# A new written order for five engines: first loads, transpose banks and the low parts of w_down in a two-layer transformer kernel

## The chip, the core and the metric

The kernel runs on one core of one Trainium2 chip. The metric is the device time of one execution in microseconds (us). The engines are TensorE (PE, with its weight loads as PEld), VectorE (DVE), ScalarE (ACT), GpSimd (POOL) and SyncE (SP), which issues the DMA transfers. Each engine works through its own list of instructions in order; semaphores make an instruction wait for data of another engine.

## The reference

Two layers, run twice with the same weights, on 2048 positions of 512 numbers, all fp32:

```python
def _A_ref(x, wqkv, wo):                    # H = 32 heads of Dh = 16
    q, k, v = split(x @ wqkv)               # wqkv: 512 x 1536
    idx = pos[:, None] - arange(8)[None] * 2 # 8 earlier positions, every second one
    logits = einsum("bhsd,bhswd->bhsw", q, k[idx]) * Dh ** -0.5   # masked where idx < 0
    o = einsum("bhsw,bhswd->bhsd", softmax(logits), v[idx])
    return o @ wo                           # wo: 512 x 512

def _B_ref(x, w_gate, w_up, w_down):        # 512 x 1792, 512 x 1792, 1792 x 512
    return (gelu(x @ w_gate) * (x @ w_up)) @ w_down

for _ in range(2):
    x = x + _A_ref(layernorm(x), wqkv, wo)
    x = x + _B_ref(layernorm(x), w_gate, w_up, w_down)
```

(The loop and the names of the split are shortened here.)

## The kernel before

**Arithmetic.** A product of fp32 matrices is made from f16 matmuls: each operand is split into a high part (the number rounded to f16) and a low part (what the rounding left), and three products high x high, high x low and low x high are added in PSUM. Weights are scaled first by a power of two, for which the largest magnitude of the weight is needed: `absmax` on DVE (L719) or `abssum` on ACT (L731) over each tile as it is loaded, then `exponents` (L615 on), which takes a turn over PE (a transpose, L628) and a few tiny DVE operations (L621, L638 to L643), then `power` (L659, L662). After that `split` makes the high part on ACT (L675) and the low part on DVE (L680). w_q has eight tiles, four for each half h of the heads; w_g and w_u have eight tiles each. The tensor names in the profile stay with a buffer, so weights that are staged elsewhere appear as w_d, bx or sc.

**w_down.** The product with w_down is done in seven block products in place of eight (a scheme of Strassen's kind). For that, `prep_d` makes seven blocks of the weight for each of seven groups u: sums on DVE (L861 to L864), a cast to f16 on ACT (L883) and the low parts on DVE (L886). For u = 0 to 4 a low part is one subtraction of 1792 elements per partition, for u = 5 and 6 two of 896.

**Stages.** The 2048 positions are eight chunks of two tiles (128 positions each), per layer. For a chunk: x tiles are loaded (L989 for the first chunk's two tiles, L971 for others), their statistics are taken on DVE (`norm`, L1035 and L1039) and finished on POOL (L1090 to L1107), ACT writes the normed tile (L1155), ACT casts the high part (L1117) and POOL subtracts the low part (L1121), and both are transposed, on PE for the first tiles (L1136, copied out of PSUM by ACT at L1143), else by a DMA of SP's (L1126). PE multiplies the transposed tile ax with w_q (L1205; for each tile and half twelve matmuls of 512 columns and twelve of 256), ACT evicts (L1231) and SP stores to a scratch in HBM (L1240), from which it fetches q and the shifted k and v (L1270). Attention is on DVE: q times k (L1293), its sum (L1302), softmax, weights times v (L1360), its sum o (L1372). o is split, transposed, multiplied with wo (L1166) and added to x (L1409). Then the feed-forward layer: norm, split, transpose (bx and hl in the profile), two matmuls (L1166), gelu on ACT (L1460), the product on DVE (L1467), block sums on POOL (L1480, L1482), cast on ACT (L1506), low part on POOL (L1511), the down product on PE (L1520), and the sums to the output on DVE (L1551). Projections of later chunks are put in front of the first feed-forward block and, later, between the blocks.

**PSUM.** During the start the pool `P_pg` for projections has six banks and the pool `P_pt` for transposes one. Some of these banks are later handed over to the accumulation of the down product; `retire` keeps them from being taken anew:

```python
P_pg = Pool(
    "pg", [ps.tile([P, 512], F32, name=f"pg{i}") for i in range(3)] + banks(pds[0], pds[1], pds[3]),
    fifo=False,
)
P_pt = Pool("pt", banks(pds[2]), fifo=False)
```

**What sets the order.** Each operation is a node of a graph (`Graph.add`), with the engine it runs on, what it reads and writes and the buffers that it takes. Nodes are numbered as they are added. `SEQ` holds a list of these numbers for each of the five engines: this list, and nothing else, is the order in which the engine issues. `Graph.plan` walks through the lists with a model of the engines' costs, to settle which buffer of a pool a node gets; it cannot change the order. Priorities and earliest times (`prio=`, `after=`) are left over from an earlier search and do not order anything here. Between the start's real work PE has a few matmuls that nobody reads (`unread`, L1594).

At the start SP's list loads four w_q tiles of half 0 first; the two x tiles of chunk 0 are its 8th and 11th transfer.

Of the kernel before, what the change touches and what calls it, by code (L numbers as in the profile page):

```python
# [39 lines left out]
    for tiles in TILES  # L40
# [15 lines left out]
    xl=-1044.97, gu=12.98, early=1, xin=554.42, wait=0.01, zero=-1577.82, dl=0, ds=0, pds=1216.47, late_end=90.68,  # L56
# [11 lines left out]

G_AT = {3: 0, 6: 1, 7: 2, 4: 3, 1: 4, 2: 5, 5: 6}
# [6 lines left out]
        17 227 228 225 226 38 96 263 271 231 298 232 230 270 229 272 274 273 275 277 276 278 279 281 280 268 282-287  # L76
        289 288 291 293 290 292 324 67 297 299 300 302 304 301 303 325 306 308 504 305 307 511 509 512 309-313 315
# [12 lines left out]
        1592 1593 1603 1604 1612 1611 1762 1620 1764 1619 1629 1599-1602 1610 1637 1630 1638 1618 1646 1645 1628  # L90
# [14 lines left out]
    """,  # L105
    "DVE": """
        13 9 16 30 18-20 240 28 34 26 250 22 24 251 241 489 491 37 492 490 58 95 39 60 59 97 40 41 63 98 64 65 45 61
        62 119 122 43 66 120 124 68 123 125 69 121 126 72 74 47 76 78 49 80 82 127 84 688 86 689-691 885 70 886 129
        340 130 131 341 135 133 342 137 887 139 888 343 141 344 143 145 345 1080 369 147 370 1081 346 176 371 1082
        178 1083 179 372 1275 182 373 348 1276 349 374 375 184 350 1277 187 1278 351 1470 352 1471 189 353 357 192  # L110
        1472 207 1473 358 1665 359 194 377 197 378 210 379 380 199 220 1667 1666 1668 381 202 382 204 386-388 213
        214 217 537 538 394 223 396 224 539-543 566 545 567 546-550 568-570 421 571 554 555 572 556 574-577 432 578
        440 579 583 584 448 450 585 736 458 737 738 591 739 593 740 764 741 765 466 474 743-748 766 482 767 483 618
        484 752 768 485 769 486 753 629 754 487 931 771 637 932 647 645 772 1860 773 1862 1863 1861 774-776 655
        780-782 933 663 934-936 959 671 960 788 790 938 961 939 940 962 963 941 942 964 943 679 680 947 681 948 682
        949 683 966 684 1126 815 1127 2057 967 2059 2058 968 826 2060 969-971 834 975-977 842 844 1128 852 1129 983
        1130 985 1154 1131 1155 1133-1137 860 1138 868 1142-1144 876-878 1156 1010 1157 879 880 1158 881 1159 1021
        1161-1164 1029 2254 2256 2255 1165 2257 1166 1039 1037 1170-1172 1321 1047 1322 1323 1055 1324 1178 1325
        1349 1326 1180 1350 1351 1063 1352 1328 1329 1353 1330-1332 1354 1333 1071 1337 1072 1338 1073 1339 1074
        1075 1356 1076 1357-1361 1365-1367 1516 1205 2449 2451 2450 2452 1517 1216 1518 1224 1519 1373 1544 1520  # L120
        1375 1545 1521 1234 1232 1523-1528 1546 1242 1547 1532 1250 1533 1548 1534 1258 1549 1711 1712 1551-1554
        1400 1411 1266 1555 1267 1268 1419 1269 1427 1429 1270 1271 1437 1445 1453 2644-2647 1461-1466 1556 2839
        1560 2840 1561 1562 1713-1715 2841 1716 2842 1739 1718 1740 1568 1719-1722 1570 1723 1741-1743 1727 1744
        1728 1729 1746-1751 1755-1757 1595 1906 1606 1907 1908 1614 1909 1763 1910 1935 1765 1936 1622 1937 1624
        1938 1939 1911 1632 1912 1940 1941 1640 1914-1917 1648 1918 1919 1923-1925 1656 1657 1943 1944 1658 1945
        1790 1659 1660 1946 1661 1801 1947 1948 1952 1953 1809 3034 3036 3035 3037 1954 1819 1817 2103-2105 1827
        1960 1962 2106 2132 1835 2133 2107 2134 2108 1843 2135 2109 2136 2137 2111 2138 2112-2116 2120 1851 1852
        2121 1853 1854 2140 1855 1856 2141 2142 2122 2143 3229 2144 3230 1987 2145 3231 2149 3232 1998 2150 2151
        2006 2300 2014 2016 2301 2302 2024 2303 2157 2328 2159 2329 2032 2304 2330-2332 2305 2040 2333 2307-2312
        2316-2318 2048 2335 2049 2336 2050 2337 2051 2338 2184 2052 2053 2339 2340 2195 2344-2346 2203 2495 2496  # L130
        2211 2213 2497 2498 2354 2499 2500 2523 2221 2524 2502 2503 2525 2526 2352 2504 2505 2229 2506 2507 2527
        2511 2512 2237 2528 2513 2530-2535 2245 2539 2246 2540 2247 2541 2248 2690 2249 2691 2250 2692 2693 2379
        2694 2718 2547 2390 2719 2695 2720 2398 2721-2723 2549 2697 2698 2406 2699 2700 2408 2701 2702 2706 2707
        2416 2708 2885 2725 2886 2726 2727 2424 2432 2728-2730 2734-2736 2887 2440 2574 2888 2441 2442 2889 2443
        2585 2913 2914 2444 2445 2593 2915 2916 2742 2744 2917 2890 2918 2601 2603 2892-2897 2901 2902 2611 2619
        2920-2922 2903 2627 2923-2925 2929 2930 2635 2931 2636 2637 2769 2638-2640 3080 2780 3081 3082 2788 3083
        2937 2939 3108 3084 3109 3085 2796 2798 3110 3087 3088 3111 3089 3112 3090 3113 2806 3091 3092 3096 2814
# [1524 lines left out]
```

## Time and profile before

| | |
|---|---|
| time, median of 3 | 1239.27 us (1238.78 to 1241.88) |
| the profiled execution | 1239.04 us |
| its span, first to last instruction | 1237.3 us |
| PE busy | 1198.5 us (97%) |
| DVE, POOL, ACT busy | 941.3 (76%), 666.8 (54%), 539.1 us (44%) |
| granted clock, mean | 0.991 |
| HBM | 115.87 MB read, 33.73 MB written |

The profile gives for each engine its busy time, for each group of instructions (line, engine, operation, tiles) the busy time, the mean of one, and the idle time in front of them with the engine whose signal ended it. A timeline row reads: start, duration, engine, line, operation, out<-in with partitions x elements, and in brackets the idle time before it. Times within the span count from its first instruction.

### The profile page before, as it was taken

The page shows a single profiled execution, that of the slowest core. Times are in us where ns is not written, and L with a number is a line of the kernel's source. Part 1 is how long each engine was busy: PE and PEld are TensorE (multiplying, and loading weights), DVE is VectorE, ACT ScalarE, POOL GpSimd, SP SyncE. Part 2 cuts the span into 40 slices and gives each one's busy share as a digit, 9 for nine tenths or more (in the row PEclk, how much of TensorE's full clock was granted, in tenths as well). Part 3 has the DMA queues.
Part 4 walks back from the last instruction along what each step waited for, and adds up shares of the span by engine and source line. Part 5 has one row for each costly group of instructions (what it writes and reads, how often), then busy time and mean ns, then how long its engine had stood idle before and what let it go on. Part 6 is the DMA issues. An engine that isn't in the chain of part 4 may idle for free. (4 is left out here: it accounts for less than half of the span.)

```text
span 1237.3 us, 23990 instructions
## 1 busy us (share of the span) xinstructions
PE 1198.5 (97%) x9722; PEld 953.7 (77%) x9722; DVE 941.3 (76%) x978; ACT 539.1 (44%) x913; POOL 666.8 (54%) x835
## 2 busy tenths in 40 slices
PE   3899999999999999999999999999999999999998
PEld 1455558887888778885678878788788888788887
DVE  6999999799778987527877768689889688866123
ACT  5887553444343426224434332524352516243321
POOL 3223427574756437562376726755376767555553
PEclk8999999999999999999999999999999999999999
DMA  9798874347434494118933455343734343341000
GB/s 353 232 287 210 211 212 140 108 149 173 154 92 127 153 235 107 44 52 228 224 107 101 133 145 168 97 146 122 213 100 130 114 137 108 117 125 44 18 18 18
DMA packets 196078, 174.75 MB, mean 141 GB/s; under 512 B 101936, under 2 KB 163200, under 8 KB 195968
## 3 DMA queue, kind: packets, MB, share of 16 engines
q1 hardware_dynamic: 195824, 173.10, 48.5%
q8 instruction: 76, 1.25, 0.4%
q14 instruction: 34, 0.28, 0.1%
q10 hardware_dynamic: 144, 0.13, 0.0%
HBM read 115.87 MB, written 33.73 MB: 121 GB/s over the span
## 5 line engine op out<-in xcount | busy, mean ns | idle before, releaser
L1166 PE MATMUL pg<-bx,w_g 128*128 128x256 f16 x2664 | 308.3, 273 | 2.6 <-DMA bx<-hl 2.1
L1166 PE MATMUL pg<-bx,w_u 128*128 128x256 f16 x2640 | 303.4, 273 | 0.5 <-DMA bx<-hl 0.4
L1166 PEld LDWEIGHTS <-w_g 128*128 128x128 f16 x2688 | 263.5, 98 | 36.5 <-DMA bx<-hl 2.9
L1166 PEld LDWEIGHTS <-w_u 128*128 128x128 f16 x2688 | 263.1, 98 | 33.2 <-issue 1.0
L1205 PEld LDWEIGHTS <-ax 128*128 128x128 f16 x1536 | 150.6, 98 | 111.2 <-issue 8.2
L1205 PE MATMUL pg<-w_q,ax 128*128 128x256 f16 (+1 forms) x1152 | 198.6, 327 | 4.8 <-ACT ax L1143 2.6
L1467 DVE SCALAR_TENSOR_TENSOR sc<-pg,small,sc 128x512 f32<-128x512 f32 (+1 forms) x126 | 84.1, 678 | 155.6 <-PE pg L1166 99.0
L1372 DVE TENSOR_REDUCE o<-prod 128x256 f32<-128x2048 f32 x64 | 146.1, 2282 | 39.0 <-POOL hl L1121 36.8
L1480 POOL TENSOR_TENSOR sc<-sc 128x256 f32<-128x256 f32 x111 | 95.2, 858 | 144.9 <-DVE sc L1467 144.6
L1460 ACT ACTIVATE sc<-pg,small 128x512 f32<-128x512 f32 (+1 forms) x127 | 79.1, 632 | 197.9 <-PE pg L1166 161.7
L1293 DVE TENSOR_TENSOR prod<-kv,q 128x2048 f32<-128x2048 f32 x64 | 156.6, 2447 | 9.3 <-DMA kv<-qkvd 7.6
L1360 DVE TENSOR_TENSOR prod<-kv,pe 128x1024 f32<-128x1024 f32 x128 | 152.1, 1215 | 1.4
L1302 DVE TENSOR_REDUCE lg<-prod 128x128 f32<-128x2048 f32 x64 | 145.7, 2277 | 0.6
L1121 POOL TENSOR_TENSOR hl<-o,hl 128x256 f16<-128x256 f32 x64 | 49.7, 777 | 123.4 <-ACT hl L1117 123.2
L1520 PE MATMUL pd<-w_d,gh 128*128 128x256 f16 x798 | 95.3, 273 | 0.0
L1511 POOL TENSOR_TENSOR w_u<-sc,w_u 128x896 f16<-128x896 f32 x37 | 80.8, 2183 | 23.8 <-ACT w_u L1506 23.8
L1520 PE MATMUL pd<-w_d,w_u 128*128 128x256 f16 x777 | 92.8, 273 | 0.6 <-POOL w_u L1511 0.6
L1520 PE MATMUL pd<-w_d,w_g 128*128 128x256 f16 x777 | 93.3, 273 | 0.0
L1511 POOL TENSOR_TENSOR w_g<-sc,w_g 128x896 f16<-128x896 f32 x37 | 75.8, 2048 | 30.2 <-ACT w_g L1506 29.0
L1482 POOL TENSOR_TENSOR sc<-sc 128x256 f32<-128x256 f32 x111 | 87.0, 784 | 8.7
L1551 DVE SCALAR_TENSOR_TENSOR x<-pd,small,x 128x512 f32<-128x512 f32 x96 | 70.2, 744 | 27.0 <-PE pd L1520 25.5
L1511 POOL TENSOR_TENSOR gh<-sc,gh 128x896 f16<-128x896 f32 x37 | 71.8, 1941 | 26.0 <-ACT gh L1506 24.9
(132 smaller groups left out, 1399.3 us busy)
## 6 DMA issues: line engine op xcount, KB each, us to landing
kv<-qkvd SPq DMA_DIRECT2D x128, 576.0 KB, 3.8
qkvd<-sc SPq DMA_DIRECT2D x64, 384.0 KB, 3.4
q<-qkvd SPq DMA_DIRECT2D x64, 128.0 KB, 3.6
x<-in_A_x_dram SPq DMA_DIRECT2D x9, 512.0 KB, 6.0
xs<-x SPq DMA_DIRECT2D x8, 512.0 KB, 3.1
xa<-xs SPq DMA_DIRECT2D x16, 256.0 KB, 4.4
x<-xs SPq DMA_DIRECT2D x8, 512.0 KB, 4.7
xa<-in_A_x_dram SPq DMA_DIRECT2D x14, 256.0 KB, 4.4
```

The source lines that it names most:

```text
L1166: nc.tensor.matmul(pt, a, b, start=i == 0, stop=i == n - 1)
L1205: nc.tensor.matmul(pgs[n].tile()[:, 0 : hi - lo], a[:, i // 2, kt], part(h * KT + kt)[:, lo:hi], start=(i, kt) == (0, 0), stop=(i, kt) == ...
L1293: nc.vector.tensor_mul(prod, win, q.tile().unsqueeze(2).to_broadcast([P, J, W, P]))
L1302: lambda lgv=lgv, heads=heads: nc.vector.tensor_reduce(lgv()[:, :, heads].rearrange("p j h w -> p j w h"), prod.rearrange("p j w (h d) -> ...
L1360: nc.vector.tensor_mul(paired[:, j].rearrange("p q (h d) t -> p q t h d", d=DH), win, by.unsqueeze(4).to_broadcast([P, W // 2, 2, HPG, DH]),)
L1372: lambda o=o: nc.vector.tensor_reduce(o.tile(), paired.rearrange("p j q c t -> p j c q t"), axis=AX.XY, op=ALU.add),
L1460: lambda sel=sel, h=h, part=part, g_of=g_of: nc.scalar.activation(g_of()[:, sel], part(0, sel), AF.Gelu_apprx_tanh, scale=cst["s_gate", h],),
L1467: lambda sel=sel, h=h, part=part, g_of=g_of: nc.vector.scalar_tensor_tensor(g_of()[:, sel], part(1, sel), cst["c_up", h], g_of()[:, sel], ...
L1480: tt(b[:, 4:6], b[:, 0:2], b[:, 3:4].to_broadcast([P, 2, P]), op=ALU.add)
L1482: tt(b[:, 1:3], b[:, 1:3], b[:, 0:4:3], op=ALU.subtract)
L1511: lambda blocks=blocks, gh_of=gh_of, cut=cut, on=nc.vector if direct else nc.gpsimd: on.tensor_sub(gh_of()[:, 1, cut], blocks()[:, cut], g ...
L1520: nc.tensor.matmul(pds_[PD_AT[m][0]].tile()[:, PD_AT[m][1]], gh_of()[:, a, G_AT[m]], wd_of(u, m, b), start=u == 0 and n == 0 and PD_AT[m][ ...
```

## The change

- **First loads.** In SP's list the two x tiles of chunk 0 become the first two transfers, then come the w_q tiles of half 0; the remaining weights and the next chunk's x follow in another order. DVE's list begins with the statistics of these tiles, and POOL's first norm stands ahead of most of what it clears to zero.
- **PSUM.** One bank goes from `P_pg` to `P_pt` (five and two).
- **w_down's low parts.** All nine subtractions go from DVE to POOL (`dl=range(7)`; the sums stay on DVE).
- **The order of all engines.** All five lists of `SEQ` are new, over the same 3432 nodes; those nine are the only ones that change their engine. The retired banks follow the new pools.
- **The planner's model** has other costs, and a term for DVE and POOL slowing each other (`HELD`). This settles buffers and emits no instruction.

The heads of the SP, DVE and POOL lists of the new version, with the numbers of the w_down subtractions (184, 189, 194, 199, 204, 213, 214, 223, 224) now on POOL, and the rest of the edit:

```diff
-    xl=-1044.97, gu=12.98, early=1, xin=554.42, wait=0.01, zero=-1577.82, dl=0, ds=0, pds=1216.47, late_end=90.68,
+    xl=-1044.97, gu=12.98, early=1, xin=554.42, wait=0.01, zero=-1577.82, dl=range(7), ds=(), pds=1216.47, late_end=90.68,
...
     "DVE": """
-        13 9 16 30 18-20 240 28 34 26 250 22 24 251 241 489 491 37 492 490 58 95 39 60 59 97 40 41 63 98 64 65 45 61
+        240 250 251 241 13 9 16 30 18-20 489 34 26 58 491 490 22 24 28 37 60 39 64 41 492 59 95 40 63 97 43 65 98
...
     "POOL": """
-        2 242 252 243 253 244 254 245 255 246 256 247 257 248 258 249 493 494 259 262 495-498 267 499 500 101 104
+        242 252 243 253 244-247 254 255 248 256 249 257-259 262 267 2 493-500 503 101 107 110 104 508 692-699 702
...
+        707 889-896 899 903 1084-1091 1094 184 1098 1279-1286 189 1293 1289 1474 1475 355 1476-1481 194 1484 361 199
+        1488 1669 204 384 1670-1676 390 213 1679 214 1683 223 224 403-409 412 416 552 422 424 558 433 441 435 581
...
     P_pg = Pool(
-        "pg", [ps.tile([P, 512], F32, name=f"pg{i}") for i in range(3)] + banks(pds[0], pds[1], pds[3]),
+        "pg", [ps.tile([P, 512], F32, name=f"pg{i}") for i in range(3)] + banks(pds[0], pds[1]),
         fifo=False,
     )
-    P_pt = Pool("pt", banks(pds[2]), fifo=False)
+    P_pt = Pool("pt", banks(pds[2], pds[3]), fifo=False)
...
+            sums_pool, low_pool = u in AT["ds"], u in AT["dl"]
...
+            sub = (nc.gpsimd if low_pool else nc.vector).tensor_sub
...
-    for q, i in ((P_pg, 3), (P_pg, 4), (P_pt, 0), (P_pg, 5)):
+    for q, i in ((P_pg, 3), (P_pg, 4), (P_pt, 0), (P_pt, 1)):
...
-    retire[2].order.extend(turns)
+    for n in retire[2:]:
+        n.order.extend(turns)
```

More of the change, by code (lines that the diff above doesn't have):

```diff
@@ L299, in start @@
         begin = max(t, self.end[e])
-        took = f * n.size / (DMA_RATE if begin > SLOW else 0.8 * DMA_RATE)
+        took = f * n.size / (DMA_RATE if begin > SLOW else 0.92 * DMA_RATE)
         both = min(max(0.0, self.end[other] - begin), 2 * took)
@@ L386, in plan, with finish @@
         free = dict.fromkeys(seq, BEGIN)
-        dma, port_free, table, cold = Transfers(), 0.0, None, COLD
+        dma, table, cold = Transfers(), None, COLD
+        busy, busy_end, dve_end = None, 0.0, 0.0
         placed = []
+        def finish(n):
+            for lease in n.uses:
+                lease.users -= 1
+                lease.free_at = max(lease.free_at, n.done)
+                if lease.users == 0:
+                    lease.pool.held[lease.slot] = None
+                    lease.pool.free_at[lease.slot] = lease.free_at
+            for m, data in n.succ:
+                if data:
+                    ready = n.done
+                    if n.eng == m.eng == "PE":
+                        ready -= LAG["PE"]
+                    elif not m.urgent:
+                        ready += MARGIN[m.eng]
+                    m.left -= 1
+                    m.ready = max(m.ready, ready)
         while len(placed) < len(nodes):
@@ L391, in plan @@
             for e, ns in seq.items():
-                if at[e] == len(ns) or ns[at[e]].left:
+                if at[e] == len(ns) or ns[at[e]].left or e == "POOL" and busy:
                     continue
                 n = ns[at[e]]
-                t = max(free[e], n.ready, port_free if n.port else 0.0)
+                t = max(free[e], n.ready)
                 if n.size is not None:
@@ L401, in plan @@
                     best = (t, n)
+            if busy and (best is None or busy_end <= best[0]):
+                busy.done, free["POOL"] = busy_end + LAG["POOL"], busy_end
+                finish(busy)
+                busy = None
+                continue
             assert best is not None, "no node can start"
@@ L423, in plan @@
             n.start = t
+            placed.append(n)
+            for m, data in n.succ:
+                if not data:
+                    m.left -= 1
+                    m.ready = max(m.ready, t + 1e-6)
+            if e == "POOL":
+                busy, busy_end = n, t + occ + HELD * min(max(0.0, dve_end - t), occ / (1 - HELD))
+                continue
+            if e == "DVE" and n.port:
+                if busy and busy_end > t:
+                    left = busy_end - t
+                    occ += 0.1 * min(occ, left)
+                    busy_end += HELD * min(occ, left / (1 - HELD))
+                dve_end = t + occ
             free[e] = t + occ
-            if n.port:
-                port_free = free[e]
             if n.size is not None:
@@ L761, in load_f @@
     def load_f(h, prio):
+        g.stage = f"f{h}"
         for k in range(KT):
@@ L816, in prep_o @@
     def prep_o(prio, how, early):
+        g.stage = "o"
         for k in range(KT):
@@ L841, in load_d @@
     def load_d(prio):
+        g.stage = "d"
         for i in range(NF):
@@ L849, in prep_d @@
     def prep_d(prio):
+        g.stage = "d"
         for f in range(NF):
@@ L884, in finish @@
                 lambda: g.add(
-                    "POOL" if AT["dl"] else "DVE port", t_pool(7 * n) if AT["dl"] else t_dve(7 * n),
+                    "POOL" if low_pool else "DVE port", (t_pool if low_pool else t_dve)(7 * n),
                     lambda: sub(lo, blocks(), hi), **rest[1],
@@ L890, in prep_d @@
         for u in range(NU):
+            g.stage = f"d{u}"
             at = prio + AT["pdu"] * u
@@ L948, in dilated_attention_geglu @@
                 ),
-                r=["zeros"], w=[("zero", l, a)], kb=60, prio=when, after=when, fixed=1.1,
+                r=["zeros"], w=[("zero", l, a)], kb=60, prio=when, fixed=1.1,
             )
@@ L1175, in attention_inputs @@
             norms = [
-                (*norm([t], prio + 100 * j - 30, "POOL", AT["mx1"] * j), 0)
+                (*norm([t], prio + 100 * j - 30, "POOL"), 0)
                 for j, t in enumerate(xt)
@@ L1256, in attention @@
             h = first // HH
+            g.stage = f"at{l}{c}{first}"
             group = range(first, first + NG)
@@ L1590, in unread @@
     def unread(k, n, **kw):
+        g.stage = "un"
         pw = Lease(P_pt)
```

221 lines of the change are left out of this document (104 added, 117 removed), and 127 rows, old and new, of the table SEQ.

## The prediction

> **What bounds the kernel now.** I read, in this order, the busy times, the busy time of PE stage by stage, what PE waited for in the first 200 us, and then the engines' timelines around each of those waits. On the page, 97% of the span is PE at work:
>
> ```profile
> PE 1198.5 (97%) x9722; PEld 953.7 (77%) x9722; DVE 941.3 (76%) x978; ACT 539.1 (44%) x913; POOL 666.8 (54%) x835
> ```
>
> The edit changes no matmul but their order, so it can only move PE's idle time. By stage (length, busy time of PE, granted clock, DMA share, GB/s):
>
> ```profile
> 0.00:50.00 50.00, 28.66 (x138) 0.86 0.89 323
> 50.00:100.00 50.00, 44.65 (x274) 0.97 0.85 252
> 100.00:200.00 100.00, 96.58 (x631) 0.98 0.76 205
> ...
> 1200.00:1238.00 38.00, 32.42 (x297) 0.96 0.04 15
> sum 1238.00, PE 1198.53; mean PE 133.17
> ```
>
> Idle are 21.3 + 5.4 + 3.4 = 30.1 us up to 200 us and 5.6 after 1200 us. What is left of the sum, 1198.53 - 28.66 - 44.65 - 96.58 - 32.42 = 996.2, says that in the thousand us between PE rests for 3.8. There is next to nothing to win there, and an advance that PE holds at 200 us is kept: the other engines feed a PE that is saturated. The question is thus how much earlier PE's list stands at the first feed-forward block. Its waits up to 200 us (total, times, longest):
>
> ```profile
> PE pd L628 <- DVE small L621: 14.0, 3, 10.9
> PE pd L1205 <- DVE w_q L680: 4.9, 2, 2.6
> ...
> PE pg L1166 <- DMA bx<-hl: 2.1, 1, 2.1
> ...
> PE pg L1205 <- ACT sc L1231: 0.9, 1, 0.9
> ```
>
> The 14.0 is loading of the first weights and their exponent; some of it stays whatever the order. The others are three gates that I follow in order of time.
>
> **Start: x first.** The timelines (start, duration, engine, line, tiles, and in brackets the idle time and who ended it):
>
> ```profile
> 6.08 0.84 ACT L731 ACTIVATE sc<-w_d 128x768 f32<-128x768 f32 x1 [4.08 <-DMA w_d<-in_A_wqkv_dram]
> 9.61 0.84 ACT L731 ACTIVATE sc<-w_d 128x768 f32<-128x768 f32 x1 [2.60 <-DMA w_d<-in_A_wqkv_dram]
> 12.77 3.41 ACT L675 ACTIVATE w_q<-w_d,small 128x768 f16<-128x768 f32 x4 [0.18 <-DVE small L662]
> 19.24 0.44 POOL L1092 TENSOR_SCALAR nw<-nw 128x1 f32<-128x1 f32 x2 [17.34 <-DVE nw L1039]
> 22.95 0.81 ACT L1155 ACTIVATE xa<-xa,nw 128x512 f32<-128x512 f32 x1 [1.90 <-POOL nw L1107]
> 27.21 0.99 ACT L1143 COPY ax<-pd 128x1024 f16<-128x1024 f16 x1
> 28.26 0.40 PE L1205 MATMUL pg<-w_q,ax 128*128 128x256 f16 x1 [1.95 <-ACT ax L1143]
> 10.00:20.00 10.00, 6.43 (x9) 2.52 (x9) 9.51 (x23) 7.35 (x15) 0.76 (x3) 0.99 1.05 398
> ```
>
> Now the norm of the first tile (19.24 to 22.95, 3.7 us) stands between weights that are ready and the first projection at 28.26. With x as SP's first two transfers the tiles are there before 6.08, when the first transfer of today lands, and the norm falls into time in which ACT waits for weights. The price is that the four weight tiles of the first half come 512 KB later: 1.3 us at the 398 GB/s of the last row. From 9.61 that gives about 11.0 for the last of them. ACT then still has, before the first projection, an abssum (0.84), four splits (3.41), two normed rows (0.81 each), two casts (1.13 together, from a row below) and two copies (0.99 each): 9.0 us, so the first projection starts near 20 instead of 28.26. That alone gains nothing: PE then eats the first half's work sooner and stands before the second half's weights.
>
> **First gate: the low part of the last w_q tile.**
>
> ```profile
> 12.02 0.15 DVE L640 TENSOR_SCALAR small<-small 128x1 int32<-128x1 int32 x1
> ...
> 12.96 0.68 DVE L1035 BATCH_NORM_STATS2 nw<-xa 128x6 f32<-128x512 f32 x1
> 40.13 0.42 DVE L638 TENSOR_REDUCE small<-pd 128x2 f32<-128x256 f32 x1 [1.60 <-ACT x L1155]
> ...
> 41.47 1.08 DVE L640 TENSOR_SCALAR small<-small 128x2 int32<-128x2 int32 x1
> ...
> 47.00 1.07 DVE L719 TENSOR_REDUCE small<-w_u 128x1 f32<-128x896 f32 x1
> 47.99 1.14 DVE L680 SCALAR_TENSOR_TENSOR w_g<-w_g,small 128x896 f16<-128x896 f32 x1
> 53.17 1.01 DVE L680 SCALAR_TENSOR_TENSOR w_q<-w_d,small,w_q 128x768 f16<-128x768 f32 x1
> 47.34 1.47 PE L1205 MATMUL pg<-w_q,ax 128*128 128x256 f16 x12
> 54.23 0.59 PE L1205 MATMUL pd<-w_q,ax 128*128 128x512 f16 x1 [2.57 <-DVE w_q L680]
> ```
>
> DVE reaches this low part at 53.17 behind a full queue. The new list puts four low parts of w_gate (4 x 1.14) and two absmax (2 x 0.99, start to start) behind it and one more bn_stats (0.68) ahead: -5.9. The 1.60 us at 40.13 is DVE waiting for an exponent's turn on PE that stands behind a projection; the new PE list has the turn ahead of it, so it goes. The start takes as much as it gives here (DVE has its first bn_stats in idle time, the weights come 1.3 later). The low part ends at 54.18 - 5.9 - 1.6 = 46.7. PE by then has one half projection less behind it, which today fills the time (1.47): the gain is 54.2 - 46.7 - 1.4 = **6.1 us**. The bounds: if the three small operations behind 40.13 shrink from the 1.08 of 41.47 to the 0.15 that the same one took at 12.02 (about 2.5 us together), 8.6; if ACT's eviction of a PSUM bank comes late because projections now share five banks instead of six (two splits of 3.41 / 4 ahead of it), 4.3. The second bank for transposes is what the sixth one was taken for: it lets the two tiles' transposes run without waiting for each other's copy (0.99), inside the 9.0 above, so I count it no second time.
>
> **Second gate: how fast the next chunks are fed.**
>
> ```profile
> 91.93 2.76 PE L1205 MATMUL pd<-w_q,ax 128*128 128x512 f16 x12 [1.07 <-DMA ax<-hl]
> 90.00:130.00 40.00, 37.60 (x224) 21.79 (x225) 37.08 (x62) 27.99 (x50) 13.69 (x30) 1.00 0.89 222
> 130.00:170.00 40.00, 39.57 (x244) 23.51 (x243) 35.76 (x44) 25.65 (x50) 14.86 (x22) 1.00 0.74 197
> L886 DVE TENSOR_TENSOR w_d<-w_d x5: 1991/2015/2024, 103.5 to 144.5; 128x1792 f16<-128x1792 f32 x5
> 1215.96 1.89 POOL L1511 TENSOR_TENSOR gh<-sc,gh 128x896 f16<-128x896 f32 x1
> ```
>
> At 91.93 PE already waits 1.07 for a transposed tile (DVE statistics, ACT, POOL, SP). Coming 6.1 earlier it would wait for it again, unless its chain moves as well. That moves by the 1.6 of the first gate and 2.2 of DVE work that now stands behind it, 3.8 less about 0.2 of POOL; and the new ACT list has its normed row ahead of some 5 us of other work, of which between nothing and 3 counts. So PE keeps between 3.6 and 6.6; I take the middle, **5.1**. Later gates bind less, since DVE (37.08 and 35.76 of 40 us, the third number after the length) gets rid of the low parts of w_down: five of 2.015 = 10.1 us by 146.5, four half-size ones (about 1.1 each) behind. They go to POOL, which is busy 13.69 + 14.86 = 28.6 of 80 us (the last number before the clock). 896 elements took POOL 1.89 beside a quiet DVE, so 1792 take about 3.6 and all nine 5 x 3.6 + 4 x 1.89 = 25.6: POOL stands at 54 of 80, and has room, as long as no low comes in front of what DVE or SP wait for.
>
> What both engines do to each other is the open cost:
>
> ```profile
> 145.10 1.91 POOL L1121 TENSOR_TENSOR hl<-o,hl 128x256 f16<-128x256 f32 x1 [2.43 <-ACT hl L1117]
> 84.95 1.80 POOL L1121 TENSOR_TENSOR hl<-xa,hl 128x512 f16<-128x512 f32 x1 [4.62 <-ACT hl L1117]
> 85.66 2.05 DVE L680 SCALAR_TENSOR_TENSOR w_u<-w_u,small 128x896 f16<-128x896 f32 x1
> ```
>
> At 1.89 per 896 elements, 256 take some 0.6; beside a low part on DVE (until 146.5) they took 1.91, so POOL stood. At 85.66 it is DVE that stood: 2.05 against 1.14. Bounds for a moved low: 3.6 on POOL and nothing on DVE, or 3.6 plus one DVE operation of 2 to 2.4, with up to 0.9 paid back by DVE each time (9 x 0.9 = 8 of 14). I take POOL's side: mostly POOL waits, as DVE is the busier one.
>
> [...]
>
> **Third gate: the first feed-forward block.**
>
> ```profile
> 179.22 4.29 PE L1166 MATMUL pg<-bx,w_g 128*128 128x256 f16 x24 [2.10 <-DMA bx<-hl]
> 186.14 2.78 PE L1166 MATMUL pg<-bx,w_g 128*128 128x256 f16 x24
> 172.63 0.60 ACT L1231 ACTIVATE sc<-pg 128x512 f32<-128x512 f32 x1 [1.50 <-DMA qkvd<-sc]
> 173.13 1.13 ACT L1117 CAST hl<-sc 128x512 f16<-128x512 f32 x2
> ```
>
> PE waits 2.10 for the transposed input, and its clock has dropped by the time it comes: 24 matmuls take 4.29 where they take 2.78 later (1.5). In ACT's queue the casts at 173.13 stand behind an eviction that itself waits 1.50 for a store; the new list has them ahead of it, and PE's list has one more half projection before this block. Together 0 to 3.8 us; I take **2.9** as the bulk of 2.10 + 1.5.
>
> **Sum.** New orders make new waits; today's bank wait is 0.9 and I charge one such, 1.0, for the five banks. 5.1 + 2.9 - 1.0 = 7.0. The profiled execution took 1239.04 (span 1237.3 and 1.7 around it), 0.2 under the median; so the forecast is **1232**, its own range 1228.5 (6.6 + 3.8) to 1235.5 (3.6 and nothing at the third gate). The tail is not touched: the same products end it.
>
> **Rivals.** *More is won*: both cap and third gate go in full and the stretched small operations too, 8.6 + 3.8 with later gates not holding: 1226.6, down to 1224 if the start is also kept. Against it: 91.93 shows how near the next gate is. *The first gate stays*: DVE is busy 9.51 of 10 us right from 10 us on, and if the low part still waits its turn (a list that puts other absmax ahead, later loads), only the third gate's smaller half is won: 1237. [...] *Slower: POOL's queue.*
>
> ```profile
> L1372 DVE TENSOR_REDUCE o<-prod 128x256 f32<-128x2048 f32 x64 | 146.1, 2282 | 39.0 <-POOL hl L1121 36.8
> ```
>
> Attention's output o has one buffer: DVE cannot reduce the next o before POOL has taken the low part of this one, and already waits 36.8 us for that over the run. The new POOL list has lows of w_down between those. If a low costs over twice its free 3.6 us, so that POOL is full (28.6 + 51 = 80 of 80), three o's come some 5 us late each: 15 lost against 10.1 won, the first feed-forward block starts 5 later, and nothing in front helps: 1244. It decides from a mean low of about 7 us.
>
> **Chances.** Forecast 0.50, more 0.10, port 0.16, gate stays 0.12, slower 0.12. A measurement here tells 0.3% (3.7 us) from nothing: under 1235.5 is faster, above 1243 slower. The port case lies on the edge and is split in half: faster 0.50 + 0.10 + 0.08 = 0.68, same 0.08 + 0.12 = 0.20, slower 0.12. The range leaves out the slower case and the lower half of "more": 1226.5 to 1239.5.
>
> **What would show it.** In the changed profile: the first L1205 near 20 instead of 28.26; the last low part of w_q (L680 on DVE) ending near 47 and PE behind it; the wait of ax<-hl near 87, not 92; w_down's low parts on POOL at 3.6 to 6 us and DVE's busy time lower by 10 to 14 us; the first 24 matmuls of the feed-forward block at 2.8, starting near 171. PE busy stays at 1197 to 1199 and its idle time falls by 7 of 39. Wrong is the prediction if PE's idle between 200 and 1200 us grows from 3.8 by several us, if that low part still ends after 52, or if lows on POOL take 7 us and o waits for them.

## The result and the profile after

The changed kernel takes 1231.36 us (median of four, 1230.9 to 1232.16) where the kernel before takes 1239.9 beside it (1238.78 to 1241.88). The ratio is 0.993, with an interval of 0.9913 to 0.9947: 8.5 us faster. The forecast was 1232. That it came out this near is in part luck: two gains were larger than forecast and one cost was larger too, which the following sections separate.

The busy times on the changed kernel's page, and its busy time of PE by stage (length, busy, granted clock, DMA share, GB/s):

```profile
PE 1195.1 (97%) x9722; PEld 950.9 (77%) x9722; DVE 940.9 (77%) x969; ACT 539.4 (44%) x913; POOL 707.2 (58%) x844
```

```profile
0.00:50.00 50.00, 32.60 (x158) 0.93 0.94 344
50.00:100.00 50.00, 46.56 (x296) 1.00 0.85 262
100.00:200.00 100.00, 98.58 (x692) 1.00 0.75 198
200.00:400.00 200.00, 200.00 (x1717) 1.00 0.48 138
...
600.00:800.00 200.00, 196.14 (x1644) 1.00 0.46 126
...
1200.00:1238.00 38.00, 24.00 (x220) 0.97 0.04 15
sum 1238.00, PE 1195.14; mean PE 132.79
```

The span is 1228.8 (8.5 less). PE is busy 3.4 us less for the same 9722 matmuls, as the granted clock of the first three stages rose from 0.86, 0.97 and 0.98 to 0.93, 1.00 and 1.00, and it is idle 33.7 instead of 38.8 us, 5.1 less. Up to 200 us the idle time is 17.4 + 3.4 + 1.4 = 22.2, where it was 30.1. But in the thousand us from 200 on, 1195.14 - 32.60 - 46.56 - 98.58 - 24.00 = 993.4 leaves 6.6 us of rest where it was 3.8. So the head won more than the end shows, and the rest gave 2.8 back.

The waits of PE up to 200 us in the changed kernel (total, times, longest). Neither the low parts of w_q (4.9 before) nor the input of the feed-forward block (2.1) is among them. The wait for the first weights and their exponent, 14.0 before, is now 6.1 and 3.1; what has grown are the waits for ACT's evictions:

```profile
PE pd L1632 <- DMA w_d<-in_A_wqkv_dram: 6.1, 1, 6.1
PE pd L652 <- DVE small L645: 3.1, 2, 2.4
PE pg L1237 <- ACT sc L1263: 2.7, 5, 0.8
PE pd L1237 <- ACT sc L1263: 2.2, 3, 1.2
PE pd L1166 <- ACT ax L1173: 2.1, 1, 2.1
...
```

The timelines of the changed kernel at the places that the prediction named: statistics of the first tile, first projection, the last low part of w_q, the first transposed tile that comes by DMA, the first feed-forward block.

```profile
3.97 0.69 DVE L1065 BATCH_NORM_STATS2 nw<-xa 128x6 f32<-128x512 f32 x1 [3.97 <-DMA xa<-in_A_x_dram]
18.97 0.38 PE L1237 MATMUL pg<-w_q,ax 128*128 128x512 f16 x1
42.52 1.01 DVE L704 SCALAR_TENSOR_TENSOR w_q<-w_d,small,w_q 128x768 f16<-128x768 f32 x1
84.61 4.07 PE L1237 MATMUL pg<-w_q,ax 128*128 128x512 f16 x24 [1.15 <-DMA ax<-hl]
169.90 2.78 PE L1196 MATMUL pg<-bx,w_g 128*128 128x256 f16 x24
```

In both kernels the same work of PE (as many matmuls of each shape) lies ahead of the last two of these rows, so that the times can be compared directly. The busy time of PE up to them, first in the kernel before, then in the changed one:

```profile
0.00:91.93 91.93, 65.24 (x363) 0.91 0.86 291
0.00:179.22 179.22, 149.11 (x866) 0.95 0.83 249
```

```profile
0.00:84.61 84.61, 63.77 (x363) 0.96 0.89 311
0.00:169.90 169.90, 147.64 (x866) 0.98 0.84 261
```

363 matmuls done: 7.3 us earlier, 1.5 of it by the clock. 866 done: 9.3 us earlier, 1.5 by the clock. Another 1.5 comes right behind, as the first 24 matmuls of the block take 2.78 instead of 4.29. These shares of the clock are those of two executions; the last section has what the others showed.

### The profile page after: what moved, and what is told of

Read it like the earlier page. It is cut to its first block, busy times and chain, and to the rows that moved or that the text cites. A ratio compares the mean times of both kernels' runs of the same rounds, so it can differ in the third digit from the quotient of the medians.

```text
span 1228.8 us, 23977 instructions
## 1 busy us (share of the span) xinstructions
PE 1195.1 (97%) x9722; PEld 950.9 (77%) x9722; DVE 940.9 (77%) x969; ACT 539.4 (44%) x913; POOL 707.2 (58%) x844
## 4 chain that ended last, share of the span: by engine, by line
PE 82%; DVE 8%; DMA 4%; POOL 3%; issue 1%; ACT 1%; SPq 1%; POOLq 0%; ACTq 0%; DVEq 0%
PE pg L1196 50%; PE pd L1556 21%; PE pg L1237 9%; DVE small L743 1%; POOL w_d L915 1%; PE pd L1237 1%; DVE w_u L704 1%; DMA ax<-hl 1%; PE pd L1196 1%; DVE prod L1326 1%; DVE lg L1335 1%; DVE w_g L704 1%; POOL hl L1151 1%; DMA qkvd<-sc 1%; DVE w_q L704 1%
## 5 line engine op out<-in xcount | busy, mean ns | idle before, releaser
L1196 PE MATMUL pg<-bx,w_u 128*128 128x256 f16 x2688 | 309.0, 273 | 1.9 <-DMA bx<-hl 1.0
L1196 PE MATMUL pg<-bx,w_g 128*128 128x256 f16 x2616 | 300.6, 273 | 2.3 <-DVE x L1443 1.8
L1237 PE MATMUL pg<-w_q,ax 128*128 128x256 f16 (+1 forms) x1176 | 202.7, 327 | 4.3 <-ACT sc L1263 3.1
L1326 DVE TENSOR_TENSOR prod<-kv,q 128x2048 f32<-128x2048 f32 x64 | 162.6, 2540 | 14.5 <-DMA kv<-qkvd 13.4
L1151 POOL TENSOR_TENSOR hl<-o,hl 128x256 f16<-128x256 f32 x64 | 58.3, 911 | 122.8 <-ACT hl L1147 119.5
L1547 POOL TENSOR_TENSOR w_u<-sc,w_u 128x896 f16<-128x896 f32 x37 | 74.0, 2001 | 31.8 <-ACT w_u L1542 31.7
L1547 POOL TENSOR_TENSOR w_g<-sc,w_g 128x896 f16<-128x896 f32 x37 | 73.3, 1982 | 30.5 <-ACT w_g L1542 30.5
L1547 POOL TENSOR_TENSOR gh<-sc,gh 128x896 f16<-128x896 f32 x37 | 75.9, 2051 | 20.7 <-ACT gh L1542 20.6
```

Of the source, the lines that this page charges most:

```text
L1196: nc.tensor.matmul(pt, a, b, start=i == 0, stop=i == n - 1)
L1237: nc.tensor.matmul(pgs[n].tile()[:, 0 : hi - lo], a[:, i // 2, kt], part(h * KT + kt)[:, lo:hi], start=(i, kt) == (0, 0), stop=(i, kt) == ...
L1326: nc.vector.tensor_mul(prod, win, q.tile().unsqueeze(2).to_broadcast([P, J, W, P]))
L1547: lambda blocks=blocks, gh_of=gh_of, cut=cut, on=nc.vector if direct else nc.gpsimd: on.tensor_sub(gh_of()[:, 1, cut], blocks()[:, cut], g ...
```

## The experiments

Times are medians, and ratios are to the kernel before on the same chip, in three batches: 1239.94 us beside h_start, h_gate1, a_lows_dve and h_after_head, 1240.91 beside h_late_x, a_banks6, b_lows_pool and h_before_head, 1240.65 beside h_gate2, after_again, h_after_head2 and h_500. Most are splices: each engine's list is the one kernel's up to a point and the other's from there. A head is the set of nodes that start before a chosen node in the planner's walk, so that it needs nothing from outside.

```diff
-SEQ = {the changed kernel's lists}
+SEQ = {e: [n for n in changed[e] if n in HEAD] + [n for n in before[e] if n not in HEAD] for e in changed}
```

### How much of the head is needed

**h_start**: HEAD ends with the first projection (90 nodes), and `dl=()` leaves the low parts of w_down on DVE.

> The lists of the changed kernel up to the first projection (x first, its norm, the first transposes, 90 nodes; five banks and two), then those of before; the low parts of w_down stay on DVE. First theory (the prediction's): the first projection starts near 19 to 20 us, and nothing of it lasts, as the second half's projections wait for the low part of the last w_q tile: 1238 to 1241 us against 1239.9. Rival 'the start itself pays': the 9 us of earlier projections pass through in good part, 1235 or less. Rival 'the relief of DVE pays': 1239 to 1240, nothing.

Measured: 1246.4 us (1244.88 to 1247.62), ratio 1.0048 (1.0032 to 1.0064). Slower, which none of the three expectations had. PE in this kernel:

```profile
19.45 0.38 PE L1231 MATMUL pg<-w_q,ax 128*128 128x512 f16 x1
...
54.71 0.58 PE L1231 MATMUL pd<-w_q,ax 128*128 128x512 f16 x1 [2.57 <-DVE w_q L698]
...
94.77 5.30 PE L1231 MATMUL pd<-w_q,ax 128*128 128x512 f16 x12 [2.04 <-DMA ax<-hl]
...
186.82 2.79 PE L1190 MATMUL pd<-bx,w_g 128*128 128x256 f16 x24 [2.08 <-DMA bx<-hl]
```

The first projection is as early as in the changed kernel, and PE stands at 54.71 before the same low part, with the same wait of 2.57 as in the kernel before (54.23). That the early start alone wins nothing up to this gate is shown. That later tiles then come later still (94.77 instead of 91.93) was not expected; the old lists with five banks and with loads in a changed order fit badly, and which of the two it is was not separated.

**h_gate1**: HEAD ends with the low part of the last w_q tile (222 nodes), `dl=()`.

> The lists of the changed kernel up to the low part of the last w_q tile on DVE (222 nodes), then those of before; low parts of w_down on DVE. First theory: that low part ends near 43.5 as in the changed kernel, PE does not wait for it, and 3.6 to 5 us last, as the second gate (91.93 in before) and the wait ahead of the first feed-forward block stay: 1234.5 to 1236.5 us. Rival 'the relief of DVE pays': 1239. Rival 'the start itself pays': the same as the kernel that has the start alone.

Measured: 1238.2 us (1235.24 to 1241.6), ratio 0.9983 (0.9969 to 0.9996), above the 1234.5 to 1236.5 of the first theory.

```profile
57.86 4.39 PE L1232 MATMUL pd<-w_q,ax 128*128 128x512 f16 x12 [3.79 <-ACT sc L1258]
...
89.77 2.76 PE L1232 MATMUL pd<-w_q,ax 128*128 128x512 f16 x12 [1.70 <-DMA ax<-hl]
...
177.31 4.42 PE L1191 MATMUL pd<-bx,w_g 128*128 128x256 f16 x24 [2.55 <-DMA bx<-hl]
```

The low part starts at 43.65 on DVE and PE no longer waits for it. But with ACT's list of before an eviction comes behind splits of w_g and w_u, abssums and a copy, and PE waits 3.79 us for the bank. The prediction had this as the lower bound of the first gate (six banks to five); here it is what happens, and 2.2 us are left at 89.77 of the 7.3.

**h_gate2**: HEAD reaches to about 95 us (441 nodes), `dl=()`.

> The lists of the changed kernel up to about 95 us (past the second gate, 441 nodes), then those of before; low parts of w_down on DVE. First theory: the first projections and the second gate are those of the changed kernel (PE waits about 1.1 us for a transposed tile near 85 us instead of 92), and the wait and the half clock ahead of the first feed-forward block are those of before: 1233 to 1236 us. If the low parts on DVE must have the new order behind them: 1237 or more, as with the splice after the last w_q tile.

Measured: 1233.91 us (1232.66 to 1236.42), ratio 0.9948 (0.9932 to 0.9963).

```profile
85.02 4.08 PE L1232 MATMUL pg<-w_q,ax 128*128 128x512 f16 x24 [1.12 <-DMA ax<-hl]
...
173.91 4.18 PE L1191 MATMUL pg<-bx,w_g 128*128 128x256 f16 x24 [2.16 <-DMA bx<-hl]
```

6.9 us are there at the second gate and 6.7 in the median, and the wait of about 2.1 stands ahead of the feed-forward block as in the kernel before, with 4.18 us for 24 matmuls behind it (4.29 there; the granted clock from 100 to 200 us is 0.98 in both). So the first two gates carry some 6.7 us. What the third adds, with the low parts, is read beside a splice that also has the lists of before behind its head, h_after_head2 below: 1229.71 in the same batch, 4.2 us less.

**h_late_x**: the other way round: lists of before up to the first projection, then the changed kernel's.

> The lists of before up to the first projection (x as 8th and 11th transfer, norm after 19 us), then those of the changed kernel. If the early start is needed though it pays nothing alone: PE's list cannot take up a start 8 to 9 us late in its waits up to 60 us (about 8 us in the changed kernel, of which those for ACT and exponents stay): 1234 to 1239 us. If only the order of DVE behind it counts: 1231 to 1233.

Measured: 1239.83 us (1237.18 to 1242.23), ratio 0.9988 (0.9971 to 1.0006): nothing clear of the noise is left of the gain.

```profile
27.93 0.40 PE L1231 MATMUL pg<-w_q,ax 128*128 128x256 f16 x1 [1.94 <-ACT ax L1167]
...
91.72 4.07 PE L1231 MATMUL pg<-w_q,ax 128*128 128x512 f16 x24 [1.11 <-DMA ax<-hl]
...
178.51 4.45 PE L1190 MATMUL pg<-bx,w_g 128*128 128x256 f16 x24 [2.10 <-DMA bx<-hl]
```

With h_start this shows two conditions of one gain: the early start and the new order behind it. Without the order the start is lost at the low part of w_q; without the start the order meets a PE that is 9 us late and rests for only 2.3 us (45.00 less 42.74 busy) between 46 and 91 us, so that there is nothing to make it up in. What the five banks do to each half was not separated.

### The banks

**a_banks6**: the changed kernel with its lists, but six banks and one.

```diff
-... banks(pds[0], pds[1])        P_pt: banks(pds[2], pds[3])   retire (P_pt, 1)
+... banks(pds[0], pds[1], pds[3]) P_pt: banks(pds[2])           retire (P_pg, 5)
```

> The changed kernel with six banks for projections and one for transposes again, all lists as in the changed kernel. First theory: the 4.9 us that PE waits for ACT's evictions up to 200 us shrink, and the first transposes wait about 1 us for the copy of the other tile: 1230 to 1233 us. Rival 'the second bank for transposes is needed for the gain': 1234 or more.

Measured: 1238.31 us (1236.08 to 1240.51), ratio 0.9982 (0.9969 to 0.9994): 7 us of the gain gone, and the expectation was wrong.

```profile
19.04 4.63 PE L1626 MATMUL pd<-w_d,ident 128*128 128x256 f32 x8 [4.32 <-ACT ax L1167]
23.46 0.69 PE L1160 MATMUL pd<-ident,hl 128*128 128x128 f16 x8
23.99 0.38 PE L1231 MATMUL pg<-w_q,ax 128*128 128x512 f16 x1
```

PE's list has matmuls that nobody reads between the transposes of the two tiles, and they write to the same pool. With one bank they wait 4.32 us until ACT has copied the first tile and run for 4.63 us (2.37 in the changed kernel; the granted clock of the first 50 us is 0.83 here and 0.93 there), and only then comes the second tile: the first projection is at 23.99 instead of 18.97. The 5.0 us are not made up: the first feed-forward block is at 177.68 instead of 169.90. The kernel has other waits behind the start as well (3.59 for DVE at 42.39), so that not each of the 7 us is traced to the bank by itself.

### The low parts of w_down

**a_lows_dve**: the changed kernel, with the nine subtractions back on DVE where POOL would start them.

```diff
-dl=range(7)   "POOL": ... 1094 184 1098 ...
+dl=()         "DVE":  each of the nine ahead of the first DVE node that starts no earlier
```

> The changed kernel with the nine low parts of w_down back on DVE, each at the place in DVE's list at which GpSimd would start it. First theory: the first two gates lie ahead of them and stay; what the 14.9 us of DVE cost shows only ahead of the first feed-forward block: 1231.5 to 1235 us, with PE waiting again by 1 to 4 us for that block's input. Rival 'the relief of DVE pays': most of the gain goes, 1236.5 to 1240. Rival 'GpSimd holds DVE for as long as it relieves it': 1231, no loss.

Measured: 1233.68 us (1232.17 to 1236.93), ratio 0.9949 (0.9931 to 0.9966). The changed kernel stands at 1231.4 and 1231.8, so the move is worth about 2 us there by the medians; the intervals of the ratios (0.9931 to 0.9966 here, 0.9913 to 0.9947 and 0.9908 to 0.9941 there) overlap, and the runs are not from one batch. Its page and the feed-forward block:

```profile
PE 1197.5 (97%) x9722; PEld 951.7 (77%) x9722; DVE 947.7 (77%) x978; ACT 539.3 (44%) x913; POOL 678.5 (55%) x835
```

```profile
172.19 2.78 PE L1190 MATMUL pg<-bx,w_g 128*128 128x256 f16 x24 [1.30 <-DMA bx<-hl]
```

The block comes 2.3 us later than in the changed kernel's profile above. That profile is an early one: in a second execution of the changed kernel (after_again, below) the block is late too,

```profile
171.55 2.78 PE L1196 MATMUL pg<-bx,w_g 128*128 128x256 f16 x24 [1.66 <-DMA bx<-hl]
```

so the profiles alone give 0.6 to 2.3 us, and the 2 us rest on the medians. The second gate is the same (84.92). And DVE is busy only 947.7 - 940.9 = 6.8 us more over the run, although nine operations with some 15 us came back. The rest had been paid all along: in the changed kernel DVE and POOL hold each other up. The five large low parts on POOL (minimum, median and maximum in ns), then the first of them with the DVE operation that starts in it, then a half-size one with the DVE operation in which it starts:

```profile
L915 POOL TENSOR_TENSOR w_d<-w_d x5: 3588/3599/3607, 93.4 to 135.6; 128x1792 f16<-128x1792 f32 x5
...
93.37 3.59 POOL L915 TENSOR_TENSOR w_d<-w_d 128x1792 f16<-128x1792 f32 x1 [0.94 <-ACT w_d L912]
93.90 4.00 DVE L704 SCALAR_TENSOR_TENSOR w_u<-w_u,small 128x896 f16<-128x896 f32 x1
...
145.75 3.24 DVE L1326 TENSOR_TENSOR prod<-kv,q 128x2048 f32<-128x2048 f32 x1
146.80 3.94 POOL L915 TENSOR_TENSOR w_d<-sc,w_d 128x896 f16<-128x896 f32 x1
```

The five large ones take 3.59 to 3.61 us on POOL, as worked out from the quiet row (3.6), and never more. The low part of w_u that DVE starts at 93.90 takes 4.00 us instead of about 1.14: it stands until POOL is done at 96.96 and ends 0.94 later. At 146.80 it is POOL that stands: DVE is at work until 148.99, and 1.75 us later the low part ends; another one of this size takes 1.88 at 157.44. So in these rows the one that came second stood until the other was done. The sums on DVE that take 1.64 us instead of 0.69 (110.69, 122.68, 131.32) run beside POOL's shorter subtractions for hl and stand for about 0.95. The five large ones never stood. As each of them began, DVE was at statistics, a reduction or weights times v, and these did not stand either: beside the large ones two of weights times v take 2.35 us (126.78 and 137.85), where the mean of one over the run is 1.22, and the reduction at 135.54 takes 2.28, as it does in the mean. What sets these operations apart from those that stood was not separated by a run.

**b_lows_pool**: the kernel before, with nothing but the nine subtractions moved to POOL (`dl=1`, and the nine numbers moved in the lists).

> The kernel before with nothing changed but the nine low parts of w_down on GpSimd, each at the place in its list at which DVE would start it. First theory: the gates at 54.2 and 91.9 us lie ahead of them and stay, and the wait ahead of the first feed-forward block is set by ACT's order: 1237 to 1240 us. Rival 'the relief of DVE pays by itself': 1235 or less. Rival 'GpSimd's queue': o waits for low parts, 1242 or more.

Measured: 1246.65 us (1242.99 to 1248.42), ratio 1.0039 (1.0022 to 1.0056): slower by 5.7, as the rival about GpSimd's queue had it (1242 or more).

```profile
103.30 3.65 DVE L1325 TENSOR_TENSOR lg<-lg,mx 128x256 f32<-128x256 f32 x1
...
125.50 2.29 DVE L1368 TENSOR_REDUCE o<-prod 128x256 f32<-128x2048 f32 x1 [1.57 <-POOL hl L1117]
131.40 0.88 DVE L857 TENSOR_TENSOR w_d<-w_d 128x256 f32<-128x256 f32 x1 [3.28 <-POOL w_d L882]
...
157.73 1.57 DVE L857 TENSOR_TENSOR bx<-bx 128x128 f32<-128x128 f32 x1 [4.31 <-ACT bx L916]
```

```profile
184.47 2.79 PE L1162 MATMUL pg<-bx,w_g 128*128 128x256 f16 x24 [1.89 <-DMA bx<-hl]
```

At 103.30 DVE stands inside an operation: it takes 3.65 us instead of 0.42, while POOL does its first large low part (103.08 to 106.67). After that DVE, whose list is still the old one, waits in front of the sums of the next group until POOL has read the last (3.28), and until ACT has scaled into a buffer that is late for the same reason (4.31); o waits 1.57. The block starts 5.3 us later than before. A low part on POOL takes 3.6 us instead of 2.0, and the chain of w_down's groups gets longer by that; the new lists start it at 93.4 instead of 103.5 us and put other DVE work in front of the sums, which leaves waits of 1.32 and 1.84 there.

### The rest of the run

**h_after_head**: HEAD ends at the first feed-forward block, low parts on POOL; then the lists of before.

> The lists of the changed kernel up to the first feed-forward block, low parts of w_down on GpSimd, then the lists of before. First theory: all of the gain lies in the head, and the 6.6 us that PE rests between 200 and 1200 us in the changed kernel go back to some 3.8: 1228 to 1230 us. Rival 'the new order of the rest pays': 1237 or more. If the rest of before does not fit the new head: 1231 to 1234.

Measured: 1229.34 us (1227.89 to 1231.06), ratio 0.9919 (0.99 to 0.9937).

**h_before_head**: the head of before, then the changed lists (low parts on DVE, six banks and one).

> The lists of before up to the first feed-forward block, low parts of w_down on DVE, six banks and one, then the lists of the changed kernel. First theory: nothing is won, and the rests of PE between 200 and 1200 us are those of the changed kernel (6.6 instead of 3.8): 1240 to 1244 us. Rival 'the new order of the rest pays': 1237 or less.

Measured: 1242.11 us (1240.06 to 1245.34), ratio 1.0009 (0.9995 to 1.0023). One stage of PE, first in h_after_head, then in h_before_head:

```profile
600.00:800.00 200.00, 199.33 (x1674) 1.00 0.46 129
```

```profile
600.00:800.00 200.00, 195.78 (x1655) 1.00 0.50 132
```

The rests of PE go with the list: 4.2 us between 600 and 800 us with the changed lists, 0.7 with those of before; from 200 to 1200 us they add up to 6.4 and 3.3. All of the gain is in the head. By the traces the new order of the rest costs some 3 us, by the medians 1.2 (h_before_head) to 2.0 us (h_after_head).

Three kernels side by side on one chip test whether the splice beats the changed kernel: **after_again** (the changed kernel), **h_after_head2** (the splice), and **h_500** (the changed lists up to about 500 us, then those of before).

> The changed kernel once more, beside the two spliced kernels that follow on the same chip: 0.993 of the kernel before, as measured first.

> The splice of the changed kernel's head (up to the first feed-forward block) with the rest of before, again, on the chip of the changed kernel. If its 1229.3 us was real: 1.5 to 3 us under the changed kernel, since PE rests 3.3 instead of 6.6 us between 200 and 1200 us; if it was another chip's difference: the same as the changed kernel.

> The lists of the changed kernel up to about 500 us, then those of before: it leaves out the changed kernel's two rests of PE at 600 to 650 us (3.9) and 850 to 900 us (1.9) and the splice's own rests of 0.95 and 1.2 us before 600 us: 1227 to 1230 us, 0 to 1.5 us under the other splice. If the rests come from what was done long before and not from the order there: the same as the changed kernel, 1231.

Measured: 1231.77 us (ratio 0.9924, 0.9908 to 0.9941), 1229.71 us (0.9913, 0.9897 to 0.9928) and 1229.24 us (0.9911, 0.9894 to 0.9929). The splices are 2.1 and 2.5 us under the changed kernel in the median, as h_after_head was before (2.0), but the intervals overlap: that the splice is faster is likely and not shown. h_500 does not add to that: it has no rest up to 400 us, and then this stage:

```profile
400.00:600.00 200.00, 196.65 (x1540) 0.99 0.54 143
```

3.35 us, where the changed lists rest 0.9 and the first splice 1.2: the seam has a rest of its own.

## Why the prediction was right, and where it was not

**What bounds the kernel** was right: nothing but the first 200 us could be won, and what was won there was kept but for the 2.8 us that the new order behind it costs. That PE's busy time would stay at 1197 to 1199 was wrong for the profiled execution: it fell to 1195.1, as waits within the first 170 us had also cost clock, which I priced at the third gate alone (1.5 of 3.4). How much of this comes back differs between executions: with the same head PE is busy for 1195.8 us in after_again, 1197.9 in h_after_head2 and 1198.7 in h_500.

**The start** was right in time (20 forecast, 18.97 measured) and in that it wins nothing alone. The prediction left out the other half: that the gain of the first gate needs it. h_late_x has the new order and wins nothing clear of the noise.

**First gate**: the low part ended at 43.5, not 46.7, a little before the early bound of that working (46.7 less 2.5): of the three small operations only one was stretched (0.94), the others took 0.17 us. PE does not wait for it at all, and is then held by ACT's evictions for 1.2 us at most. The lower bound, the late eviction (by its own terms 4.4, not 4.3), shows in h_gate1, where ACT has the old list.

**The second bank for transposes** I counted at nothing, hidden in the start's 9.0 us; with the new PE list it is a condition of that start. The wait for the other tile's copy is not 0.99 but 4.3 of waiting and 4.6 of unread matmuls behind it; it makes the start 5.0 us later, and the kernel is 7 us slower at the end. The step failed since I asked what waits for a bank among transposes only, not what else in PE's list writes to that pool.

**Second gate**: 5.1 was forecast (3.6 to 6.6), 7.3 measured. The wait is there, 1.15, as it was 1.07: the chain through DVE, ACT and POOL moved by as much as PE did. I had capped it by what I could add up of DVE's and ACT's shifts; the new lists moved more ahead of other work than that.

**Third gate**: 2.9 forecast. From the second gate to the first block PE wins another 2.0 (7.3 to 9.3), and 1.5 by the clock behind it: 3.5. With the old lists behind the second gate the wait stays (2.16 in h_gate2, and 4.18 us for the first 24 matmuls); with the low parts the third gate is worth 4.2 by the medians of h_gate2 and h_after_head2. It is not gone for good: in the second execution of the changed kernel it is 1.66, but the 24 matmuls take 2.78. The 1.5 for the clock was read from one execution, and waits of about 2.1 us did not all cost it (last section).

**Low parts of w_down**: POOL's load was right: 26.55 + 27.77 = 54.3 of 80 us busy between 90 and 170, against 54 worked out, though with two errors that cancel: the nine low parts took 29.2 instead of 25.6, the rest of POOL's work 25.1 instead of 28.6. These are the windows of the changed kernel; the numbers after the length are PE, its weight loads, DVE, ACT and POOL:

```profile
90.00:130.00 40.00, 39.98 (x245) 23.71 (x244) 34.64 (x49) 28.41 (x49) 26.55 (x27) 1.00 0.80 203
130.00:170.00 40.00, 38.60 (x226) 21.85 (x225) 37.71 (x40) 24.88 (x49) 27.77 (x28) 1.00 0.76 212
```

Which engine stands was wrong. I took it that POOL would mostly wait; the five large ones never did, and DVE paid back 8 of some 15 us. That is the size of the other bound (8 of 14), but not made up of nine times 0.9: one low part of w_u stood for 2.9 us, other operations for 0.3 to 1.7. DVE's busy time over the run fell by 0.4, not by 10 to 14, as q times k also got longer (162.6 instead of 156.6 us over the run). That is the new order, since it is 162.3 in a_lows_dve too. The holds went in both directions: DVE stood until POOL's low part was done (4.00 us at 93.90, and 3.65 at 103.30 in b_lows_pool), and POOL until DVE was done (3.94 us at 146.80).

**New waits** at 1.0: too small. The bank waits stayed within the head's account, but the new order of the rest costs 2.8 us between 200 and 1200; that the rests go with the list is shown by the two splices. So the sum 5.1 + 2.9 - 1.0 = 7.0 stands against 7.3 + 3.5 - 2.8 = 8.0 by the same points, with 8.5 in the span: two terms too small and a cost too small.

**The rivals**: the slower one names the right engine, and happens when the low parts are moved alone (b_lows_pool, 5.7 slower; 1244 worked out), mostly by a different queue as far as the trace tells: DVE's sums behind POOL's low parts (3.28 and 4.31), and o's wait the smaller part (1.57). It came without the condition that I gave: a low part did not have to take 7 us, 3.6 were enough. The port case (0.16) has its part in what happened to DVE: it was held for up to 2.9 us in one operation (4.00 less 1.14), but the third gate was not lost. That a port lies behind the holds no run shows: the runs show which operations stood, and for how long.

## What to carry to other kernels

Where one engine is saturated but for its first stage, compare two kernels at the points where that engine has done the same work: the difference there is the gain, and every rest behind it is read from the list's own stages. A chain of gates is not a sum of independent terms: test each with the other's half, since a start that is early and an order that uses it can each be worth nothing alone. And before counting an operation as moved off an engine, look for who is held beside it and who stands in line behind the new, longer one: the same move was 5.7 us slower with the old lists and about 2 us faster, not clear of the noise, with new ones.

## What the runs showed that was not expected

- DVE and POOL held each other up, and of some pairs of operations the one that came second stood until the other was done. Inside POOL's low parts of 3.59 us a low part of w_u on DVE took 4.00 instead of 1.14 us (93.90 in the changed kernel) and a subtraction of the softmax 3.65 instead of 0.42 (103.30 in b_lows_pool); half-size low parts on POOL took 1.88 us beside a reduction (157.44 in the changed kernel), and 3.94 and 3.50 where DVE was at q times k first (146.80 and 153.97). DVE's reductions (2.28 us) and weights times v (2.35 us for two) ran on beside POOL's large low parts at their usual length. So what the move cost went with which operations stood beside each other in the lists.
- Matmuls that nobody reads were not free where they share a PSUM pool: with one bank for transposes instead of two (a_banks6) they held PE's list for 4.3 us and ran for 4.6.
- What a wait cost in clock went by where it fell, not by its length alone. After waits of 1.30, 1.66, 1.89, 2.06 and 2.08 us ahead of the first feed-forward block (a_lows_dve, after_again, b_lows_pool, a_banks6, h_start) the 24 matmuls took 2.78 or 2.79 us; after 2.10, 2.10, 2.11, 2.16 and 2.55 (before, h_late_x, h_before_head, h_gate2, h_gate1) they took 4.18 to 4.46. That looks like a step between 2.08 and 2.10 us, and is none: in the granted clock's record of each of the two kernels all changes lie whole multiples of 3.41 us apart (half clock from 19.89 to 33.55, 54.03 to 57.44 and 180.32 to 183.73 in the kernel before, from 34.47 to 41.30 in the changed one), and two of the cases are seen to differ in the work of PE within such a stretch. Two stretches of the kernel before, then two of h_start (length, busy, clock, DMA share, GB/s):

```profile
176.91:180.32 3.41, 1.31 (x12) 1.00 0.77 192
180.32:183.73 3.41, 3.41 (x18) 0.50 1.02 261
...
182.17:185.58 3.41, 2.58 (x12) 1.00 0.85 257
185.58:188.99 3.41, 2.17 (x20) 1.00 0.69 179
```

  In the kernel before all of the wait lies in one stretch, 1.31 us of work are left in it, and the next stretch is at half clock. In h_start a wait of nearly the same length (2.08) is spread over two, with 2.58 and 2.17 us of work, and the clock stays at 1.00. A stretch with 1.46 us of work lost it too: in h_start the 12 matmuls behind the wait of 2.04 at 94.77 took 5.30 us, where they take 2.76 at 91.93 in the kernel before. Where the border lies, and whether it is sharp, is not shown. The stretches do not start with the kernel: counted back by whole ones, one began 2.8 us after the first instruction in the kernel before (from 19.89) and 0.3 in the changed one (from 34.47). So a wait of about 2.1 us cost 1.4 to 1.7 us in some of these executions and nothing in others.
